# Infini-attention beside grouped attention: segment 3's memory is asked inside the attention, and the last q tile is split behind the flag

## The chip, the cores and the metric

The kernel runs on one core of a Trainium2 chip. The metric is the device time of one launch in microseconds, as the median of several runs; all matrices go in and come out in float32.

## What is computed

Two attention layers work on their own inputs, and their outputs are put side by side. Both have S = 2048 tokens, D = 576, 32 heads of 18.

```python
# A: all heads share one k and one v
scores = einsum("bhqd,bkd->bhqk", q, k) * Dh ** -0.5
a = merge(einsum("bhqk,bkd->bhqd", softmax(scores), v)) @ wo

# B: four segments of 512 tokens, causal inside a segment, with a memory of the segments before
phi = lambda t: where(t > 0, t + 1.0, exp(t))
for s in range(4):
    p = softmax(einsum("bhqd,bhkd->bhqk", qs, ks) * scale + mask)
    a_dot = einsum("bhqk,bhkd->bhqd", p, vs)
    num = einsum("bhld,bhde->bhle", phi(qs), M)              # the memory is asked
    den = einsum("bhld,bhd->bhl", phi(qs), z)[..., None] + 1e-6
    o = g * (num / den) + (1.0 - g) * a_dot
    M = M + einsum("bhld,bhle->bhde", phi(ks), vs)
    z = z + sum(phi(ks), "l")
b = merge(o) @ wo
```

Segment 0 has an empty memory. Segments 1, 2 and 3 ask it: a numerator of 18 values for each head and token, and a denominator.

## The kernel before, in words

**Two stages.** The first makes all projections: A in four chunks of 512 tokens, then B in four segments. Heads lie seven to a tile (126 rows; the fifth tile has four heads, 72 rows), so q of a segment is five tiles t = 0 to 4. Each result is split exactly into two parts (`split2`: a rounding cast on ScalarE, a subtraction on VectorE) and stored to DRAM (`store_parts`). The second stage is the attention, which loads stacks of eight heads back from DRAM. Between the two stands a branch on `flag`: if a bound on the scores is too loose, exact maxima are computed first. With these inputs that part is skipped, but each engine reads the flag and branches, and at the branch SP waits until all DMAs issued before it from the hardware queues are counted, for both ways have to leave the semaphores alike.

**The end of the first stage (segment 3, `last`).** For each q tile t = 0 to 3 (lines 527 to 539): project into one of four PSUM buffers `pj`, take the absolute value (`magnitude`), split, store to `qB`, then `phi` (Relu and Exp on ScalarE, one VectorE operation) and `from_memory`. Then come the denominators (541 to 550), the bound matmuls `pu` (554), the reduction to `fm` (555), `loose_flag`, the shifts (`shift_parts`, stored to `shB`), and `values(i, 1)`: the second half of v in four groups of 14 matmuls, each copied by ScalarE and stored to `vB` from ScalarE's queue. PE, ACT and DVE take these in the order that a scheduler gives them; `pin` and `keep_in_program_order` hold some where the program has them.

**Asking the memory.** There are two ways. Segment 3 asks in the first stage: `from_memory` multiplies `phi(q)` by the memory `Mst` (429), weighs the result by the gate (433) and stores it to `numB`; lines 545 to 550 make the denominators. Segments in `LATE_ASK`, (1, 2), only store `phi(q)` to `qfB` and their memory to `mzB` (426, 597, 598). In the attention `ask_memory` works them off: six pairs of steps for a segment (t = -1 for the denominators, then the five tiles), each step four matmuls of 256 columns on a 32-column strip (826) into the one PSUM buffer F. A pair ends with one or two VectorE reads (831, 835), and two turns later the stores to `numB` and `denB`. `asked[0]` says which segment is done.

**The attention's order** is written out by hand for PE, ACT and DVE. Work is cut into blocks of four heads, `("A", chunk, group)` or `("B", segment, group)`, and these into turns k of up to three items: 416 turns, 11 for a block of A, two for a block of B. In a turn stand the scores of three items (PE, 919 for A and 928 for B), their exponentials (ACT, 937; one of three from a copy W that VectorE makes, 934), one step of other work, and the products of the turn before the last (PE, 967). The step of other work is one of `ask_memory` until that is through, then one of the output projection (`run_fill`, 770):

```python
if memory is None:
    run_fill()
elif k >= ASK and all(its[n][0] == "A" for n, pr in turns[k]) and next(memory, None) is None:
    memory = None
```

So asks stand in turns of A only, from k = ASK = 20 on.

**Buffers and due times.** `later` is a list of steps with the turn from which they are due and a condition (`at`, `due`). The pool tile "o" has two buffers. `load_qf(s)` loads `phi(q)` of a segment into one, and the output projection's `parts` take the same two afterwards. `load_qf(1)` stands ahead of the turns, `load_qf(2)` is due at k = 24. `place()` lets a finished block take a buffer for its heads only once enough segments are asked. All loads and stores of the attention go through SP's queue, in order.

## Time and profile before

| | us |
|---|---|
| median of 3 runs | 1421.37 (1420.92 to 1422.42) |
| the profiled execution, its own time | 1422.46 |
| its span, from first to last instruction | 1420.8 |
| first score of the attention (PE) | 292.81 |
| busy in the span: PE / ACT / DVE / POOL | 1404.1 / 1205.0 / 1034.9 / 248.5 |
| mean granted clock of TensorE | 0.998 |

Times in rows are microseconds from the span's start. A row of the time line gives start, duration, engine, line, operation, output and input, count, and in brackets how long the engine had been idle and what released it. A row of groups gives the count, then the busy time in us and the mean of one in ns. A row of a stretch gives its bounds and length, the busy time of PE, weight loads, DVE, ACT and POOL with counts, the granted clock, the DMA share and GB/s. In a row of a line's instructions stand the shortest, median and longest duration in ns and the first and last start. Matmuls are pipelined, so their durations overlap; what one costs is read from starts.

### The profile page before, as it was taken

What the parts mean: (1) busy time and instruction counts of PE and PEld (TensorE: products, weight loads), DVE (VectorE), ACT (ScalarE), POOL (GpSimd) and SP (SyncE); (2) the same over time, 40 slices, a digit from 0 to 9 for tenths busy, and PEclk for the clock granted to TensorE, in tenths of its full rate; (3) what the DMA queues carried; (4) which work ended last, traced back from release to release, by engine and by line L of the source; (5) the groups of instructions that cost most, each with busy time, mean ns of one, the idle gap of its engine ahead of it and who ended that gap; (6) DMA issues with size and microseconds to landing.
All of it is one profiled execution on the core that took longest, in us unless ns stands there. A gap on an engine that the chain in (4) does not pass through costs nothing.

```text
span 1420.8 us, 40029 instructions
## 1 busy us (share of the span) xinstructions
PE 1404.1 (99%) x17132; PEld 844.8 (59%) x17132; DVE 1034.9 (73%) x1220; ACT 1205.0 (85%) x1448; POOL 248.5 (17%) x326
## 2 busy tenths in 40 slices
PE   9999999999999999999999999999999999999998
PEld 6788888745555555555555555555555555555558
DVE  6656456467787778877777888777778877887773
ACT  4543434479999999999999999999999999999991
POOL 2431000003313214221110160131011400100002
PEclk9999999999999999999999999999999999999999
DMA  9866546467565535332312542232104121110013
GB/s 271 268 207 187 166 144 219 168 175 223 154 212 160 168 117 162 90 113 77 111 58 70 165 131 91 67 107 75 51 34 135 64 75 47 59 44 18 9 60 111
DMA packets 90720, 172.63 MB, mean 122 GB/s; under 512 B 14576, under 2 KB 22889, under 8 KB 90110
## 3 DMA queue, kind: packets, MB, share of 16 engines
q1 hardware_dynamic: 83978, 159.75, 35.9%
q0 software_dynamic: 1664, 4.78, 1.3%
q10 hardware_dynamic: 4896, 5.51, 1.1%
q8 instruction: 135, 2.21, 0.7%
q14 instruction: 47, 0.39, 0.1%
HBM read 99.32 MB, written 70.67 MB: 120 GB/s over the span
## 4 chain that ended last, share of the span: by engine, by line
PE 67%; ACT 9%; issue 2%; DVE 1%; DMA 0%; POOL 0%; ACTq 0%; DVEq 0%
PE O L967 30%; PE E L919 19%; PE F L770 11%; ACT P L937 9%; PE E L928 3%; PE E L1164 2%; PE F L826 1%; DVE W L934 0%; DMA oA<-oe 0%; PE F L1164 0%; PE O L1164 0%; DMA sm<-oA 0%; POOL P L942 0%; DVE osb L794 0%; DVE o L831 0%
## 5 line engine op out<-in xcount | busy, mean ns | idle before, releaser
L937 ACT ACTIVATE P<-E 128x1024 f32<-128x1024 f32 (+1 forms) x800 | 781.7, 1062 | 11.7 <-PE E L919 11.6
L934 DVE COPY W<-E 128x1024 f32<-128x1024 f32 (+1 forms) x384 | 461.0, 1200 | 176.3 <-PE E L919 120.1
L967 PE MATMUL O<-P,VA 128*32 128x256 f32 x7936 | 508.3, 379 | 0.0
L937 ACT ACTIVATE P<-W 128x1024 f32<-128x1024 f32 (+1 forms) x384 | 427.9, 1114 | 3.9 <-DVE W L934 3.7
L967 PEld LDWEIGHTS O<-P,VA 128*32 128x32 f32 x7936 | 262.6, 110 | 146.5 <-issue 5.7
L919 PE MATMUL E<-stA,kstA 56*128 56x512 f32 x1920 | 329.0, 439 | 2.3 <-DVE W L934 1.3
L919 PEld LDWEIGHTS E<-stA,kstA 56*128 56x128 f32 x1920 | 154.9, 184 | 178.1 <-ACT P L937 112.4
L942 POOL TENSOR_SCALAR_AFFINE_SELECT P<-P 128x256 f32<-128x256 f32 (+1 forms) x192 | 94.6, 493 | 474.0 <-ACT P L937 441.5
L758 POOL TENSOR_TENSOR o<-o,rb 126x512 f32<-126x512 f32 (+1 forms) x55 | 81.9, 1504 | 410.2 <-DMA o<-oA 263.8
L770 PE MATMUL F<-woB,o 126*32 126x192 f32 (+1 forms) x1920 | 127.4, 338 | 0.3 <-DVE osb L794 0.3
L899 DVE SCALAR_TENSOR_TENSOR q<-q,PD 128x1024 f32<-128x1024 f32 x96 | 120.3, 1253 | 0.0
L967 PE MATMUL O<-P,vseg 128*32 128x256 f32 (+2 forms) x1536 | 81.8, 344 | 0.4 <-issue 0.3
L770 PEld LDWEIGHTS F<-woB,o 126*32 126x32 f32 (+1 forms) x1920 | 38.2, 108 | 70.7 <-issue 62.7
L976 DVE COPY oe<-O 128x512 f32<-128x512 f32 x64 | 44.2, 691 | 40.7 <-PE O L967 40.0
L249 PE MATMUL pj<-xh,wBl 128*126 128x512 f32 x180 | 72.4, 403 | 0.0
L249 PE MATMUL pj<-xh,wBh 128*126 128x512 f32 x180 | 71.8, 400 | 0.0
L118 ACT CAST qp<-pj 126x512 fp32r<-126x512 f32 (+1 forms) x54 | 30.9, 584 | 44.7 <-DVE kmB L447 32.9
L770 PE MATMUL F<-woA,o 126*32 126x192 f32 (+1 forms) x960 | 63.9, 338 | 0.0
L967 PEld LDWEIGHTS O<-P,vseg 128*32 128x32 f32 x1536 | 49.0, 109 | 24.9 <-issue 2.0
L928 PE MATMUL E<-stB 56*128 56x256 f32 (+3 forms) x512 | 61.2, 347 | 1.3 <-ACT P L937 0.9
L119 DVE TENSOR_TENSOR qp<-pj,qp 126x512 fp32r<-126x512 f32 (+1 forms) x54 | 36.6, 684 | 35.4 <-ACT qp L118 35.2
L249 PE MATMUL pj<-xl,wBh 128*126 128x512 f32 x144 | 57.3, 399 | 0.0
(193 smaller groups left out, 1388.6 us busy)
## 6 DMA issues: line engine op xcount, KB each, us to landing
stB<-kB SPq DMA_DIRECT2D x96, 144.0 KB
stB<-qB SPq DMA_DIRECT2D x32, 288.0 KB
stA<-qA SPq DMA_DIRECT2D x30, 288.0 KB
oA<-oe SPq DMA_DIRECT2D x32, 256.0 KB
oB<-oe SPq DMA_DIRECT2D x32, 256.0 KB
qA<-qp SPq DMA_DIRECT2D x16, 504.0 KB
kB<-qp SPq DMA_DIRECT2D x16, 504.0 KB
qB<-qp SPq DMA_DIRECT2D x16, 504.0 KB
```

The costliest lines, as they stand in the source:

```text
L119: hold(nc.vector.tensor_tensor(qp[:R, 1, :n], src, qp[:R, 0, :n].bitcast(F32), op=ALU.subtract))
L249: nc.tensor.matmul(dst, w[:, c0 : c0 + M], x, start=i == 0, stop=i == len(ops) - 1)
L758: return lambda: tc.keep_in_program_order(nc.gpsimd.tensor_tensor(dst, a, b, op=op))
L770: nc.tensor.matmul(dst[32 * j : 32 * j + 32], parts[ab, c][: RT[t], t, r0 : r0 + 32], wo[ab][: RT[t], t, c0 : c0 + n], start=start, stop=stop,
L899: steps.append(lambda a=a: v.scalar_tensor_tensor(q, q, a, p, op0=ALU.add, op1=ALU.mult))
L919: nc.tensor.matmul(e[:, j], kstA[rows, 128 * kt : 128 * kt + 128], st[rows, h, :], start=True, stop=True)
L928: nc.tensor.matmul(e[:, j, c0 : c0 + 512 - 128 * k], st[rows, 4 + h, ks], st[rows, h, 128 * k :], start=True, stop=True)
L934: nc.vector.tensor_copy(src[:, :, :n], e[:, :, :n])
L937: nc.scalar.activation(p[:, :, :n], src[:, :, :n], AF.Exp, scale=SCALE)
L942: nc.gpsimd.affine_select(diag, diag, pattern=[[0, 2], [0, m], [1, 128]], base=0, channel_multiplier=-1, compare_op=ALU.is_ge, fill=0.0)
L967: nc.tensor.matmul(o[32 * j : 32 * j + 32, q0 : q0 + n], v, p[:, j % 2, p0 : p0 + n], start=m == hf == 0, stop=last and hf == 1,)
L976: nc.vector.tensor_copy(osb, o)
```

## The change

Segment 3 joins `LATE_ASK`. It stores `phi(q)` in place of numerators, from POOL's queue instead of SP's; its matmuls, gate multiplications and denominators leave the first stage. In segment 3 the last q tile (t = 3) is only projected and its absolute value taken in the loop; its split, store, `phi` and `from_memory` come behind `loose_flag`.

In the attention 36 steps of `ask_memory` are worked off instead of 24. A turn may now take one if its items are of A, or if the products that it takes (of the turn two before) are of the same kind as its items. The third `load_qf` becomes due at k = 32 once segment 1 is asked, and is issued three turns later, into the buffer that segment 1's q had; the buffer's stores must have landed. `place()` lets the first finished block load its heads once two segments are asked, the second once three are.

```diff
-LATE_ASK, ASK = (1, 2), 20
+LATE_ASK, ASK = (1, 2, 3), 20
...
             def from_memory(t):
                 R = RT[t]
                 if s in LATE_ASK:
-                    nc.sync.dma_start(qfB[s][:R, t], fs[t][:R])
+                    (nc.gpsimd if last else nc.sync).dma_start(qfB[s][:R, t], fs[t][:R])
                     return
...
                 proj(pj[:126], wBh, wBl, xh, xl, 126 * t, 126)
                 magnitude(t, pj)
+                if last and t == 3:
+
+                    lastq = pj
+                    continue
                 qp = split2(pt, pj[:126], 126)
                 store_parts(qp, 0, 126, qB[s], 7 * t, 7)
...
             if last:
                 loose_flag()
+                qp = split2(pt, lastq[:126], 126, pin)
+                store_parts(qp, 0, 126, qB[s], 21, 7)
+                fs[3] = phi(lastq[:126], 126, "qf", 5, pin)
+                from_memory(3)
             sp = shift_parts(pt, pu, -BOUND_UP, C, 128)
             sent = nc.sync.dma_start(shB[s].rearrange("j r t -> r j t"), sp.bitcast(F32))
...
         def place():
 
-            return (ab, c) in parts or len(parts) - filled[0] // FILL < 2 and asked[0] >= min(2, len(parts) + 1)
+            return (ab, c) in parts or len(parts) - filled[0] // FILL < 2 and asked[0] >= min(3, len(parts) + 2)
...
         at(ASK + 4, 0, lambda: True, lambda k: load_qf(2))
 
+        at(ASK + 12, 0, lambda: asked[0] >= 1, lambda k: at(k + 3, 0, lambda: True, lambda k: load_qf(3)))
+
...
             if memory is None:
                 run_fill()
-            elif k >= ASK and all(its[n][0] == "A" for n, pr in turns[k]) and next(memory, None) is None:
+            elif k >= ASK and its[turns[k][0][0]][0] in ("A", its[prods[k - 2][0][0]][0]) and next(memory, None) is None:
+
                 memory = None
```

## The prediction

> **What bounds the kernel now.** I read the page's busy time and slices first, then stretches of the time line around the three places that the change touches.
>
> ```profile
> PE 1404.1 (99%) x17132; PEld 844.8 (59%) x17132; DVE 1034.9 (73%) x1220; ACT 1205.0 (85%) x1448; POOL 248.5 (17%) x326
> ...
> PE   9999999999999999999999999999999999999998
> ...
> ACT  4543434479999999999999999999999999999991
> ```
>
> Two stages stand there. Up to the eighth slice (some 290 us) PE is full and ACT half idle: the projections, bound by PE. From the ninth slice PE and ACT are both full: the attention, where one of them is the bound in each kind of turn and the other is close behind. The change takes PE work out of the end of the first stage and puts it into the second.
>
> **PE work that leaves the first stage.** Segment 3 loses five numerator matmuls (L429) and five denominator matmuls (L545).
>
> ```profile
> L429 PE MATMUL mm<-qf,Mst 126*126 126x512 f32 (+1 forms) x10 | 5.2, 602 | 0.0
> ...
> L545 PE MATMUL nd<-qf,zst 126*32 126x512 f32 (+1 forms) x10 | 3.4, 602 | 0.0
> ...
> L554 PE MATMUL nd<-aq,kbB 126*32 126x512 bf16 (+1 forms) x5 | 1.0, 386 | 0.0
> ```
> ```profile
> 274.27 0.39 PE L249 MATMUL pj<-xl,wBh 128*126 128x512 f32 x1
> ...
> 274.50 0.40 PE L249 MATMUL pj<-xh,wBl 128*126 128x512 f32 x1
> ...
> 274.74 1.02 PE L429 MATMUL mm<-qf,Mst 126*126 126x512 f32 x2
> ...
> 275.83 0.40 PE L249 MATMUL pj<-xl,wBh 128*126 128x512 f32 x1
> ...
> 285.22 1.05 PE L545 MATMUL nd<-qf,zst 126*32 126x512 f32 x4
> ...
> 286.20 0.27 PE L396 MATMUL nd<-ident,fm 128*1 128x128 f32 x1
> ```
>
> Matmuls overlap, so I price them by starts. Two projection steps take 2 x 0.23 (274.27 to 274.50); from 274.50 to 275.83 there are two of them and one L429, so an L429 holds PE for 1.33 - 0.46 = 0.87, and five for 4.35 us. Each is recorded as two rows, hence x10. Four of the ten L545 rows take 286.20 - 285.22 = 0.98; all ten at that rate 2.45. Together 6.8 us; the busy columns (5.2 + 3.4) cap it at 8.6, and 4.35 alone is the floor. VectorE loses six operations here, which nobody on this path waits for any more.
>
> **A wait that appears.** In the changed program's order the last q tile keeps its PSUM buffer until behind the flag, so the second group of `values` must take the buffer of the second q tile. That is free only after ScalarE has done four operations behind the last projection (absolute value, Relu, cast, Exp) and VectorE two.
>
> ```profile
> L388 DVE SCALAR_TENSOR_TENSOR qf<-pj,ph_e 126x512 f32<-126x512 f32 x5 | 3.4, 679 | 1.1 <-ACT ph_e L386 1.1
> L118 ACT CAST qp<-pj 126x512 fp32r<-126x512 f32 x6 | 3.3, 590 | 0.5 <-ACT kn L495 0.4
> L386 ACT ACTIVATE ph_e<-ph_e 126x512 f32<-126x512 f32 x5 | 3.1, 629 | 0.1
> ...
> L385 ACT ACTIVATE ph_e<-pj 126x512 f32<-126x512 f32 x5 | 3.0, 593 | 3.1 <-DVE qp L119 3.1
> ```
> ```profile
> 289.58 0.40 ACT L493 COPY vch<-pj 128x288 f32<-128x288 f32 x1 [1.47 <-PE pj L491]
> ...
> 290.01 0.33 ACTq L496 DMA_DIRECT2D vB<-vch  x1
> ...
> 291.12 0.29 PE L491 MATMUL pj<-wBl,xh 128*128 128x288 f32 x1
> ...
> 291.45 0.40 ACT L493 COPY vch<-pj 128x288 f32<-128x288 f32 x1 [1.47 <-PE pj L491]
> ...
> 292.81 1.16 PE L919 MATMUL E<-st,kstA 56*128 56x512 f32 x6 [1.41 <-SPq L607]
> ```
> ```profile
> L607 SPq EVENT_SEMAPHORE  x8: 17/17/17, 292.1 to 292.6; - x8
> ```
>
> The chain takes 0.59 + 0.59 + 0.59 + 0.63 (taking the absolute value as long as the Relu) and then 2 x 0.68, about 3.8 us. In it PE has one group of `values`, 1.87 us (copies at 289.58 and 291.45), and four of the five bound matmuls of L554, 0.8. So PE waits 1.1 us (0 to 1.8). Net on PE so far: 6.8 - 1.1 = 5.7 us earlier at its last `values`.
>
> **The handover.** The bracket at 292.81 says what released the attention: SP's eight semaphore events at the branch, 292.1 to 292.6. They follow stores: the third `vB` store went out at 290.01, so a store takes about 2.1 us to be counted. The fourth is issued behind the branch and holds nobody. Before, PE went idle at 291.41 and started at 292.81, 1.40 later. In the changed order all four `vB` stores stand ahead of the branch. Behind PE's end there now come the copy 0.40, the store 2.1, three events of 0.07 (eight took 0.5; this store counts on the sixth of the eight semaphores) and 0.2 to PE's start, with small gaps 2.95. That gives back 1.55: 5.7 - 1.55 = 4.1.
>
> SP's branch waits for other stores too: the last q tile and the shifts now leave behind the flag. By the built order the flag is written beside the third group of `values`, some 1.4 groups or 2.6 us ahead of the last `vB` store.
>
> ```profile
> 288.00:290.00 2.00, 2.00 (x17) 2.00 (x16) 0.00 (x0) 0.51 (x2) 0.00 (x0) 1.00 1.05 400
> ```
> ```profile
> qB<-qp SPq DMA_DIRECT2D x4, 504.0 KB
> ...
> vB<-vch ACTq DMA_DIRECT2D x5, 152.0 KB
> shB<-shp SPq DMA_DIRECT2D x1, 512.0 KB
> ```
>
> 504 + 512 + 3 x 152 and one `qfB` store (126x512 floats, 252 KB) make 1.72 MB. At 400 GB/s that is 4.3 us, against 2.6 + 2.1 = 4.7 to the count of the last `vB` store; with the start-up of the burst it lands 0 to 0.9 us later than that. I take 0.4, so the attention starts 3.7 us earlier (bounds: 2.5 and 5.2, the latter without wait and burst). `qfB` moves from SP to POOL. The Trainium skill (Trainium Kernel Development and Optimization, Key Constraints) says that the queues of SP, ACT and POOL run on the same 16 DMA engines. By that the 252 KB stay in the burst; with a path of its own for POOL it would be 0.6 us shorter. The DMA share of 1.05 in the row fits, but shows no POOL store.
>
> **The asks in the attention.** Twelve steps are added, four matmuls each. By the built order they stand so that eight more fall into turns of B and four more into turns of A, of which two had no step; the output projection starts two turns later and makes both up in turns that were empty, with the same three steps left at the end.
>
> ```profile
> 309.32 1.98 ACT L937 ACTIVATE P<-E 128x1024 f32<-128x1024 f32 x2
> ...
> 312.07 2.00 ACT L937 ACTIVATE P<-E 128x1024 f32<-128x1024 f32 x2
> ...
> 379.50 1.78 ACT L937 ACTIVATE P<-E 128x1024 f32<-128x1024 f32 x2
> ...
> 388.81 2.07 ACT L937 ACTIVATE P<-E 128x1024 f32<-128x1024 f32 x2
> 391.10 1.94 ACT L937 ACTIVATE P<-E 128x1024 f32<-128x1024 f32 x2 [0.22 <-PE E L919]
> ...
> 466.94 1.72 ACT L937 ACTIVATE P<-E 128x1024 f32<-128x1024 f32 x2
> ...
> 476.35 1.94 ACT L937 ACTIVATE P<-E 128x1024 f32<-128x1024 f32 x2
> 478.84 1.94 ACT L937 ACTIVATE P<-E 128x1024 f32<-128x1024 f32 x2 [0.55 <-PE E L919]
> ```
> ```profile
> 348.67 0.64 PE L826 MATMUL F<-o,woA 126*32 126x256 f32 x8
> 349.13 1.48 PE L967 MATMUL O<-P,VA 128*32 128x256 f32 x24
> ...
> 351.44 0.64 PE L826 MATMUL F<-o,woA 126*32 126x256 f32 x8
> ...
> 462.44 0.53 PE L770 MATMUL F<-woB,o 126*32 126x192 f32 x8
> 462.79 1.37 PE L967 MATMUL O<-P,vseg 128*32 128x256 f32 x24
> ```
>
> A turn of A lasts 312.07 - 309.32 = 2.75 without a step and 351.44 - 348.67 = 2.77 with an ask: 0.02 each, 0.1 for all. A pair of B turns without a step lasts (388.81 - 379.50) / 2 = 4.65, paced by ACT. With steps of the output projection, 0.35 each (462.44 to 462.79), it lasts (476.35 - 466.94) / 2 = 4.70, paced by PE, and ACT's gap at the next turn of A grows from 0.22 to 0.55. An ask holds PE for 0.46 (348.67 to 349.13), 0.11 more than those: the pair becomes 4.92, 0.27 over 4.65. Four pairs: 1.1. Two stretches end in a gap that is 0.2 to 0.3 longer: 0.5. Sum 1.7 us, bounds 0 (PE's lead covers all) and 12 x 0.46 = 5.5. VectorE takes seven more short reads of F beside its 27% idle time: nothing, up to 1 if they delay a copy that ACT waits for. The third q's load stands behind stores issued three turns earlier, so SP's queue, with the stacks behind it, waits for what has landed: nothing.
>
> **The clock.**
>
> ```profile
> 296.60:300.00 3.40, 3.40 (x26) 1.49 (x30) 3.40 (x4) 3.40 (x5) 0.00 (x0) 0.50 0.72 170
> ```
>
> The granted clock is 0.50 in these 3.4 us, soon after the gap, and ACT stays full. PE's gap now grows from 1.4 to some 3.3 us. A second such stretch would meet turns of which PE needs 2.77 - 0.46 = 2.31 at full clock, 4.62 at half, against 2.75: a loss of 3.4 x (1 - 2.75 / 4.62) = 1.4. I take 0.2 of 0 to 1.4. The Trainium skill (TensorE: Matmul & The Clock Gate, What's actually happening) has the clock halved after an idle window of about 3.4 us; by it a second slow window is possible here, not certain, and would cost that 1.4.
>
> **Sum.** -3.7 + 1.7 + 0.2 = -1.8 us. The profiled execution took 1422.46 (its span 1420.8 and 1.66 around it), 1.09 over the median of the three runs, so it would be 1420.7, and the median 1421.37 becomes 1419.6 us.
>
> **The rivals.** What a measurement of this kernel can tell from no change is about 0.2%, 2.84 us.
> Faster: the asks hide and the early work is worth all of its price. The start gains its bound 5.2, the asks cost 0.8: -4.4, 1417.0. For it: PE's own work in a pair is 4.70 - 0.70 = 4.0 of the 4.65. Against it: the 0.35 steps already show at 4.70.
> Slower: the handover becomes bound by transfers. If the 1.72 MB at the branch run at 200 GB/s instead of 400, they take 8.6 us, 4.3 more: the start gains -0.6, and with 1.7 and 0.2 the time is 1421.4 + 2.5 = 1423.9. It decides from 3.7 us more, that is below some 215 GB/s. Against it stand the 400 GB/s, with nearly the same stores; for it, that the burst is the largest of the stage and now stands directly ahead of the start.
> The change doing nothing of what it says is no rival: the built order has the matmuls moved.
>
> **How the numbers follow.** The forecast of -1.8, with terms that leave it within 2.84, gets 0.58. Faster gets 0.30, since 1 us less of wait, burst or asks suffices. Slower gets 0.12, with the load of the third q or the upper bound of the asks beside the burst. Range: the forecast's own terms reach from 1418 to 1422; stretched to the faster case's 1417.0 and towards 1423.9 it is 1416.8 to 1423.0.
>
> **What would show it.** Right: no L429 in segment 3's end, PE's first score near 289, its gap before it 3 us or more, released by SP's branch; B pairs with asks at 4.9. Wrong: the first score at 291 or later, B pairs still at 4.65, a long wait of PE for `qf`, or a slow clock stretch of 7 us.

## The result: 1425.4 us, 0.26% slower

| | before | after |
|---|---|---|
| median of 8 runs each, on one chip | 1421.3 (1420.8 to 1423.5) | 1425.4 (1422.2 to 1429.7) |
| ratio after / before, 95% interval | | 1.0026 (1.0016 to 1.0035) |
| profiled execution: own time / span | 1422.46 / 1420.8 | 1424.54 / 1422.8 |
| mean granted clock | 0.998 | 0.995 |

The forecast was 1419.6 with a range to 1423.0: the wrong sign, and outside the range. The page of the changed kernel, its busy time and two of its slices:

```profile
PE 1401.0 (98%) x17208; PEld 845.2 (59%) x17208; DVE 1036.2 (73%) x1221; ACT 1205.5 (85%) x1448; POOL 248.9 (17%) x331
...
PE   9999999989999999999999999999999999999998
...
PEclk9999999989999999999999999999999999999999
```

The totals do not say where the time went: PE is busy 3 us less in a span that is 2 us longer. The ninth slice of PE and of its clock, where the handover lies, has an 8. To see the rest one needs a ruler. VectorE's first operation on the scores of A (`PD<-E`, line 892 before, 900 after) starts each block of A. The table has its starts in both traces and the time since the start before. The last column has the names that the experiments use: the stretch from the first to the second start is the "first block", and each later stretch has the name of the start that ends it.

| start of block of A | before | after | after - before | time since the last, before | after | called in the experiments |
|---|---|---|---|---|---|---|
| 1 (turn 0) | 293.94 | 291.12 | -2.82 | | | |
| 2 (turn 19) | 340.65 | 338.85 | -1.80 | 46.71 | 47.73 | first block |
| 3 (turn 38) | 388.52 | 387.93 | -0.59 | 47.87 | 49.08 | third block |
| 4 (turn 53) | 427.58 | 430.40 | +2.82 | 39.06 | 42.47 | fourth block |
| 5 (turn 72) | 476.52 | 480.22 | +3.70 | 48.94 | 49.82 | fifth block |
| 32 | 1348.42 | 1352.30 | +3.88 | | | |

So 2.8 us are won at the start, 1.0 and 1.2 are lost in the next two stretches, 3.4 between turns 38 and 53, 0.9 behind that, and next to nothing more for 870 us. (The span grew by only 2.0 because the profiled execution of before took 1.9 us longer from start 32 to its end; the medians differ by 4.1, the last row of the table by 3.9.)

**1.45 of the 2.8 us are not the change's.** PE's first matmuls of the kernel stay longer at about half their later pace in some executions than in others. Before, and after:

```profile
6.77 2.06 PE L281 MATMUL pj<-xh,wAh 128*114 128x512 f32 x4 [1.21 <-ACT wAh L222]
8.62 0.63 PE L281 MATMUL mm<-xh,wAh 128*126 128x512 f32 x1
```
```profile
6.71 1.19 PE L281 MATMUL pj<-xh,wAh 128*114 128x512 f32 x4 [1.16 <-ACT wAh L222]
7.74 0.39 PE L281 MATMUL mm<-xh,wAh 128*126 128x512 f32 x1
```

Four matmuls take 1.85 us in the one (8.62 - 6.77) and 1.03 in the other, in the same order. From some 20 us up to 270 us, where the change begins, the traced execution of before is 1.1 to 1.5 us later at the same matmuls (191.38 against 189.93, for one). Call the one a late beginning and the other an early one. Both are found with both first stages among the kernels of the experiments. Between traces that begin alike, the changed stage has PE's last values 5.3 to 6.2 us earlier, the first score 2.1 to 3.3 and the first start 1.0 to 2.4: that is what the change wins at the start.

**The stretch that loses 3.4 us.** What the engines waited for between 300 and 484 us (in total, how often, the longest), before:

```profile
ACT P L937 <- DVE W L934: 1.0, 3, 0.4
```

and after:

```profile
ACT P L945 <- DVE W L942: 5.3, 3, 3.7
...
PE E L927 <- DVE W L942: 2.8, 3, 1.5
DVE sm L734 <- DMA sm<-oB: 2.6, 1, 2.6
...
PE F L834 <- DMA o<-qfB: 1.6, 1, 1.6
```

The time line of the changed kernel there, each engine's rows that have a wait, with the releaser in brackets:

```profile
411.35 0.64 PE L834 MATMUL F<-o,woA 126*32 126x256 f32 x8 [1.56 <-DMA o<-qfB]
...
412.88 0.95 DVE L734 RECIPROCAL sm<-sm 112x128 f32<-112x128 f32 x1 [2.63 <-DMA sm<-oB]
...
415.44 1.06 ACT L945 ACTIVATE P<-W 128x1024 f32<-128x1024 f32 x1 [3.72 <-DVE W L942]
...
415.46 0.50 PE L927 MATMUL E<-stA,kstA 56*128 56x512 f32 x2 [1.52 <-DVE W L942]
```

VectorE's order is written out by hand. In it the reciprocal of B's first sums waits for their load (2.63 us); behind the reciprocal stands the copy W that ScalarE's next exponential needs (3.72 us of waiting), and then TensorE has no free scores buffer (1.52 us). The chain of the changed kernel goes through the same load (start, us, what):

```profile
394.22 6.56 DMA stA<-qA
400.80 12.05 DMA sm<-oB
412.88 0.96 DVE sm L734
...
414.18 1.22 DVE W L942
```

SyncE's queue shows what is new ahead of it. Before:

```profile
395.22 0.40 SPq L880 DMA_DIRECT2D vseg<-vB  x1
396.90 0.86 SPq L713 DMA_DIRECT2D sm<-oB  x1
```

After:

```profile
396.09 0.83 SPq L888 DMA_DIRECT2D vseg<-vB  x1
397.55 0.34 SPq L811 DMA_DIRECT2D o<-qfB  x1
398.88 0.32 SPq L812 DMA_DIRECT2D o<-qfB  x1
400.80 1.93 SPq L721 DMA_DIRECT2D sm<-oB  x2
402.77 8.76 SPq L710 DMA_DIRECT2D woB<-b_wo  x5
```

The third q's load (1.15 MB) now stands between B's values (1.2 MB) and the sums (64 KB). Before the change the sums were issued 8.4 us after the third start (396.90 - 388.52), and VectorE took their reciprocal at 407.78 without a wait. After the change they were issued 12.9 us after that start, and took 12.05 us to land.

One more thing moved. The list of small steps takes at most two in a turn (`most=2` in `due`). In the changed kernel the third q's load takes one of the two places of turn 39, so the step that loads the sums goes from turn 39 to turn 40, and the reciprocal, five turns behind it, from turn 44 to 45. VectorE comes to it 22.3 us after the third start (412.88 - 2.63 - 387.93) where it came after 19.3 before the change (407.78 - 388.52). The later place gave the sums 3 us more time; the wait is what was left in spite of it.

**The start.** The changed handover, rows of PE and of ScalarE, then two stretches:

```profile
284.13 0.29 PE L491 MATMUL pj<-wBl,xh 128*128 128x288 f32 x1
...
284.89 0.73 ACTq L496 DMA_DIRECT2D vB<-vch  x1
...
288.94 0.46 PE L927 MATMUL E<-st,kstA 56*128 56x512 f32 x1 [4.52 <-DMA vB<-vch]
289.74 1.61 PE L927 MATMUL E<-st,kstA 56*128 56x512 f32 x5 [0.33 <-SPq L615]
...
290.81 3.88 ACT L945 ACTIVATE P<-E 128x1024 f32<-128x1024 f32 x4 [5.95 <-SPq L615]
```
```profile
284.00:286.00 2.00, 0.42 (x4) 0.18 (x2) 0.00 (x0) 0.40 (x1) 0.00 (x0) 1.00 0.99 334
286.00:288.00 2.00, 0.00 (x0) 0.00 (x0) 0.00 (x0) 0.00 (x0) 0.00 (x0) 1.00 1.00 320
```

PE ends 7.0 us earlier (284.4 against 291.4), the first score comes 3.9 earlier, the first exponential 2.7 (293.55 before), each with the 1.45 in it. Between the end of PE's work and the first score the transfer engines are full (shares 0.99 and 1.00) at 320 to 334 GB/s.

### The profile page after: what moved, and what is told of

Same layout as the page of the kernel before. It is cut to its first block, busy times and chain, and to the rows that moved or that the text cites. A ratio compares the mean times of both kernels' runs of the same rounds, so it can differ in the third digit from the quotient of the medians.

```text
span 1422.8 us, 40185 instructions
## 1 busy us (share of the span) xinstructions
PE 1401.0 (98%) x17208; PEld 845.2 (59%) x17208; DVE 1036.2 (73%) x1221; ACT 1205.5 (85%) x1448; POOL 248.9 (17%) x331
## 4 chain that ended last, share of the span: by engine, by line
PE 67%; ACT 7%; issue 2%; DMA 2%; DVE 1%; SPq 1%; ACTq 0%; DVEq 0%
PE O L975 31%; PE E L927 19%; PE F L778 11%; ACT P L945 7%; PE E L936 3%; PE E L1175 2%; DMA sm<-oB 1%; PE F L834 1%; DMA stB<-qB 0%; DMA stA<-qA 0%; DVE W L942 0%; PE F L1175 0%; PE O L1175 0%; SPq L701 0%; SPq L847 0%
## 5 line engine op out<-in xcount | busy, mean ns | idle before, releaser
L984 DVE COPY oe<-O 128x512 f32<-128x512 f32 x64 | 44.2, 691 | 39.8 <-PE O L975 37.6
L118 ACT CAST qp<-pj 126x512 fp32r<-126x512 f32 (+1 forms) x54 | 31.0, 584 | 45.3 <-DVE kmB L447 33.1
L119 DVE TENSOR_TENSOR qp<-pj,qp 126x512 fp32r<-126x512 f32 (+1 forms) x54 | 36.6, 685 | 35.6 <-ACT qp L118 35.6
```

Of the source, the lines that this page charges most:

```text
L119: hold(nc.vector.tensor_tensor(qp[:R, 1, :n], src, qp[:R, 0, :n].bitcast(F32), op=ALU.subtract))
L984: nc.vector.tensor_copy(osb, o)
```

## The experiments

Theory 1: the third q's load makes B's sums late, and VectorE's order passes that on. Rival 1: the asks, in turns of B above all, cost TensorE the time. Rival 2: the longer pause at the handover costs clock. All numbers of blocks are from one profiled execution each, which can lie some us beside the median of its kernel; the medians are of 4 to 12 runs. The kernels ran on several chips, on which the kernel before had medians from 1421.2 to 1422.1; the ratios are each to before on the same chip. Of the traces in the table, before, "no third load" and "asks held" have the late beginning, the others the early one. "Keys" is the issue of the last piece of B's next keys on SyncE's queue, counted from the fourth start; it is explained further below.

| kernel | median | ratio to before (95%) | first start | first | third | fourth | fifth block | keys |
|---|---|---|---|---|---|---|---|---|
| before | 1421.3 | | 293.94 | 46.71 | 47.87 | 39.06 | 48.94 | 25.9 |
| after | 1425.4 | 1.0026 (1.0016-1.0035) | 291.12 | 47.73 | 49.08 | 42.47 | 49.82 | 33.1 |
| early q | 1428.6 | 1.0060 (1.0041-1.0078) | 291.41 | 47.32 | 49.08 | 45.33 | 48.98 | 29.9 |
| late sums | 1422.4 | 1.0010 (1.0000-1.0021) | 290.80 | 47.59 | 49.08 | 40.53 | 48.98 | 34.6 |
| two segments, asks in B | 1421.3 | 1.0004 (0.9995-1.0014) | 292.91 | 47.00 | 49.12 | 38.98 | 48.30 | 26.8 |
| no third load | 1423.5 | 1.0010 (1.0001-1.0020) | 292.96 | 47.57 | 49.13 | 39.76 | 49.49 | 32.5 |
| early q, late sums | 1425.4 | 1.0029 (1.0016-1.0042) | 291.18 | 47.73 | 49.12 | 39.12 | 52.94 | 36.5 |
| weights late | 1425.3 | 1.0025 (1.0013-1.0036) | 290.53 | 47.79 | 49.10 | 40.03 | 49.83 | 35.6 |
| late sums, weights late | 1422.7 | 1.0009 (0.9995-1.0024) | 290.96 | 47.74 | 49.10 | 39.56 | 49.38 | 35.3 |
| the same, asks held | 1428.3 | 1.0044 (1.0031-1.0056) | 292.48 | 47.67 | 49.10 | 38.75 | 56.84 | 39.8 |
| q on GpSimd's queue | 1426.5 | 1.0029 (1.0018-1.0040) | 291.17 | 47.74 | 49.11 | 44.06 | 49.67 | 32.5 |
| the same, late sums | 1426.2 | 1.0026 (1.0015-1.0037) | 291.69 | 47.37 | 49.10 | 39.03 | 55.83 | 38.7 |
| sums two turns late | 1424.6 | 1.0019 (1.0010-1.0028) | 291.15 | 47.21 | 49.09 | 41.18 | 48.84 | 33.1 |
| the same, weights late | 1428.1 | 1.0048 (1.0034-1.0062) | 291.12 | 47.74 | 49.10 | 40.00 | 53.08 | 37.0 |

**The reciprocals three turns later (late sums).**

```diff
-... (2, 5, 3, 5) if (ab, c) == ("B", 0) ...
+... (2, 8, 3, 5) if (ab, c) == ("B", 0) ...
```

> The load of B's first sums stays where it is, and the reciprocals that read them are asked of VectorE three turns later. Theory 1: VectorE's wait at the reciprocal (2.6 us) and the waits of ScalarE on W (3.7) and TensorE on W (1.5) in 410 to 416 us go; what stays is TensorE's 1.6 us for the q of the asks. The fourth block's loss falls from 3.4 to about 1.5 us, the time to about 1423.3. Rivals 1 and 2: no part of the loss hangs on the reciprocal, 1425 stays.

Measured: 1422.4, 3.0 under the changed kernel by the medians, 2.3 by the ratios. VectorE has no wait at the reciprocal, the fourth block is 40.5, and TensorE's wait for q is what is left:

```profile
PE F L834 <- DMA o<-qfB: 1.6, 1, 1.6
```

As theory 1 said, and neither rival: only the reciprocal, the deadline of the sums, was moved, with the steps that follow from it.

**No third load.**

```diff
+        if s == 3:
+            nc.gpsimd.memset(qfs[s], 1.0)
+            return
         nc.sync.dma_start(qfs[s][:126, :4], qfB[s][:126, :4])
```

> Leaves out part of the computation: the third segment's q is not loaded (1.15 MB less on SyncE's queue), GpSimd fills the tile with ones in its place, and everything else, the asks too, is as in the changed kernel. Theory 1 as the first runs leave it (wherever the load stands ahead of the sums, its bytes and its turn on SyncE's queue make the sums late): the load of the sums lands some 6 us after its issue and not after 12, VectorE does not wait at the reciprocal, TensorE does not wait for q, and the fourth block's loss of 3.4 us falls under 0.5; about 1421.5. Rival 1 (the asks themselves, in turns of B and in the third segment, cost TensorE the time): at most the 1.6 us of the wait for q goes, 1423.8 or more.

Measured: no wait at the reciprocal and none for q, and the fourth and fifth block together are 4.3 - 1.25 = 3.0 us shorter than after's. The sums are issued 9.4 us after the third start, though their step stands in turn 40 here too: of the 4.5 us by which the changed kernel issued them later, the load itself made 3.5. The median is 1423.5, 2 us over the expectation. (The trace has the late beginning, which says nothing of the median: PE's last values start at 285.83 and not 284.13, with the same order of matmuls.) So the load costs 1.9 us by the medians, 2.3 by the ratios, and without it the change would still not pay: 1.0010 (1.0001 to 1.0020). The 36 asks run in full here, so rival 1 has at most 1.25 of the 4.3 us.

**Two segments, asks in turns of B.** The kernel before with the new condition of turns alone:

```diff
-elif k >= ASK and all(its[n][0] == "A" for n, pr in turns[k]) and next(memory, None) is None:
+elif k >= ASK and its[turns[k][0][0]][0] in ("A", its[prods[k - 2][0][0]][0]) and next(memory, None) is None:
```

> The kernel before with only the new condition of turns: its two segments ask B's memory in turns of B too; no third q, first stage untouched. Rival 1: the asks in turns of B by themselves cost their time on TensorE beyond what they displace, about 1.2 us (6 asks), so 1422.5. Theory 1: no cost that is not the load's: no wait of VectorE for the sums over 0.5 us, the same time as before within 0.5 us (1421.3).

Measured: the same time, 1.0004 (0.9995 to 1.0014). The third block is 1.25 us longer, by six asks, and the fourth and fifth are 0.7 us shorter, since fewer are left for them. Asks in turns of B take 0.2 us each (1.25 / 6), and 0.7 of the 1.25 comes back; rival 1 falls as an explanation of 4 us. (This trace has the early beginning, so that its first start is 1.0 us earlier than before's with the same first stage.)

**The third q's load three turns earlier (early q).**

```diff
-at(ASK + 12, 0, lambda: asked[0] >= 1, lambda k: at(k + 3, 0, lambda: True, lambda k: load_qf(3)))
+at(ASK + 12, 0, lambda: asked[0] >= 1, lambda k: load_qf(3))
```

> The third q's load (1.2 MB) is put on SyncE's queue three turns earlier, ahead of the values' load and not between it and the load of the sums. Theory 1 (the load sits right before the sums of B, whose landing then takes 12 us; VectorE waits for them at the reciprocal, and behind that stand the copies W that ScalarE's next exponential needs): the wait of VectorE at the reciprocal goes from 2.6 us to under 0.5, the stretch from the third to the fourth block loses 0 to 1 us against before in place of 3.4, and the time is about 1422.0 us. Rival 1 (the asks in turns of B cost TensorE its time) and rival 2 (the longer pause at the handover costs clock): the stall is by chance beside that load, nothing of the loss goes, 1425.

Measured: 1428.6, three us worse. TensorE no longer waits for q, and VectorE waits longer:

```profile
DVE sm L734 <- DMA sm<-oB: 4.0, 1, 4.0
```

A miss, and not for the reason that comes to mind first. Here the third q's load leaves turn 39, so the reciprocal is back in turn 44. VectorE's rows ahead of it, here:

```profile
405.32 1.21 DVE L907 SCALAR_TENSOR_TENSOR q<-q,PD 128x1024 f32<-128x1024 f32 x1
410.57 0.95 DVE L734 RECIPROCAL sm<-sm 112x128 f32<-112x128 f32 x1 [4.03 <-DMA sm<-oB]
```

and in the changed kernel, where a copy W, two reads of F and this row stand between the same two:

```profile
409.55 0.69 DVE L909 TENSOR_SCALAR n<-n 128x1024 int32<-128x1024 f32 x1
```

VectorE comes to the reciprocal 18.7 us after the third start in place of 22.3. The sums are issued later than in the changed kernel (14.4 us after the third start, behind values that the load makes late), and yet they land sooner, 22.8 us after it in place of 24.9. So moving the load did bring the sums forward by 2.2 us; what was lost is the later deadline, 3.6 us. Theory 1 had to be put wider: 1.15 MB more anywhere ahead of the sums makes them late, and the wait is their landing less their deadline.

**Both together.** The two edits above in one kernel.

> The early load of the third q and the late reciprocals together. If it is the deadline of the sums that decides, the wait of 4.0 us that the early load alone showed at the reciprocal is covered by the three turns, and TensorE's wait of 1.6 us for q goes as well: fourth block's loss under 0.5 us, 1421.0, under the late reciprocals alone (1422.4). If the early load costs by what it does to the other loads ahead of it (the states of A, the values), it stays over 1423.

Measured: 1425.4. The fourth block is as before the change (39.1), as expected, and the fifth takes 52.9, 4 us longer than before. TensorE has a new wait of 2.2 us for B's next queries: the gain moved on. What that is, the runs further below show.

**Queue or room.** First the output projection's weights, queued behind the sums, ten turns later:

```diff
-load_wo(*(("B", b_wo) if it[2] == 2 else ("A", a_wo)))
+if it[2] == 2:
+    at(k + 10, 0, lambda: True, lambda k: load_wo("B", b_wo))
+else:
+    load_wo("A", a_wo)
```

> The changed kernel; only the five loads of the output projection's weights (1.3 MB, issued right behind the load of the sums, needed 20 turns later) are put ten turns later. Theory 1a, order: the sums are late because the third q's 1.15 MB and the values stand ahead of them, and what is queued behind them does not matter: the load still takes 12 us, VectorE waits 2.6 us at the reciprocal, the fourth block loses its 3.4 us, 1425. Theory 1b, room: all loads in flight share the engines, and 3.6 MB between 396 and 416 us are too many: with 1.3 MB gone the sums land in 7 to 8 us and q 2 us sooner, the waits at the reciprocal and for q fall under 1 us each, the fourth block loses under 1 us, 1422.5.

Measured: in the profile the sums land 10.0 us after their issue in place of 12.05, just in time,

```profile
409.92 0.95 DVE L734 RECIPROCAL sm<-sm 112x128 f32<-112x128 f32 x1 [0.18 <-DMA sm<-oB]
```

and the fourth block loses 1.0. But that execution took 1421.85, the least of ten; their median is 1425.3. With the sums 0.2 us from too late, most executions seem to fall on the other side, which no trace here shows. Undecided. Then the load went off SyncE's queue, with its bytes and its turn kept. Theory 2a is that the place in SyncE's queue makes the sums late, 2b that the bytes in flight do:

```diff
-        nc.sync.dma_start(qfs[s][:126, :4], qfB[s][:126, :4])
-        nc.sync.dma_start(qfs[s][: RT[4], 4], qfB[s][: RT[4], 4])
+        q = nc.gpsimd if s == 3 else nc.sync
+        q.dma_start(qfs[s][:126, :4], qfB[s][:126, :4])
+        q.dma_start(qfs[s][: RT[4], 4], qfB[s][: RT[4], 4])
```

> The changed kernel; only the third q's load goes through GpSimd's queue in place of SyncE's, at the same turn, when GpSimd stands idle (392 to 420 us). Theory 2a (SyncE's queue: it issues in order, and each issue waits for the landing of one some eight issues earlier, so that a long load ahead delays the issue of all that follow): the sums are issued some 8.5 to 9.5 us after the third block's start as before the change, not 12.9, VectorE does not wait at the reciprocal, the fourth block loses 0.5 to 1.5 us, 1422.5. Theory 2b (the room of the transfer engines): the same bytes fly in the same stretch, the sums land as late, the wait of over 2 us at the reciprocal stays, 1425.

Measured: 1426.5. GpSimd issues the load at 394.63, ahead of the values (395.93), where SyncE had issued it behind them. The first sums are issued 10.2 us after the third start, 2.7 sooner than in the changed kernel, and they land no sooner:

```profile
398.21 11.23 SPq L721 DMA_DIRECT2D sm<-oB  x2
```
```profile
413.17 0.95 DVE L734 RECIPROCAL sm<-sm 112x128 f32<-112x128 f32 x1 [2.31 <-DMA sm<-oB]
```

From 398.21 to some 413 are 15 us, and VectorE waits 2.3. Between the two loads of sums, SyncE's queue itself waits for a store of B's outputs to land:

```profile
SPq L721 <- DMA oB<-oe: 9.7, 1, 9.7
```

So 2a fails and it is as 2b said: what is in flight holds the sums, and not only the place in SyncE's queue. (The values were ahead of them on that queue in both kernels.) The Trainium skill (DMA: Bandwidth & Descriptors, Queues, rings and completion order) says that a transfer's count lands only after every earlier write of that DMA engine, across its queues. The trace agrees as far as it goes: 56 KB from SyncE's queue were counted 15 us after their issue, with 1.15 MB of another queue and 1.2 MB of their own in flight.

**Later deadlines and more room.**

Late reciprocals (three turns) and late weights in one kernel:

> The late reciprocals and the late loads of the weights together. By 1b q lands in time too, and TensorE's 1.6 us for it, which the late reciprocals alone left, go: fourth block under 0.5 us later than before's, 1421.0 and so about even with the kernel before. By 1a q still lands 13 us after its issue and the 1.6 us stay: 1422.4 as with the late reciprocals alone.

Measured: 1422.7, as the late reciprocals alone (1422.4). TensorE's wait for q falls from 1.6 to 0.7 in the profile; the time does not show it. To these two edits comes a hold of the third segment's asks:

```diff
         for s in LATE_ASK:
+            while s == 3 and now[0] < 48:
+                yield False
             qf = qfs[s]
```

> As the run before, and the third segment's asks are held until turn 48 (two turns later). If q is what TensorE still waits for, the hold takes the rest of that wait away whatever the loads do: no wait of TensorE for q over 0.3 us, 1420.5 to 1421.5, the fastest of the versions. If the hold only moves the asks to where they cost the same, it equals the run before.

Measured: 1428.3. The wait for q is gone and the fourth block is the shortest of all, 38.75; the fifth takes 56.8.

The load on GpSimd's queue with the reciprocals three turns late:

> The third q's load on GpSimd's queue and the reciprocals three turns later. By both theories there is no wait at the reciprocal; what the late reciprocals alone left was 1.6 us of TensorE for q. By 2a q is issued and lands sooner, and B's queries, behind it on SyncE's queue, too: 1421.0 to 1421.7, even with the kernel before. By 2b it is as the late reciprocals alone, 1422.4.

Measured: 1426.2, again with a fourth block as before the change (39.0) and a fifth of 55.8. Then the reciprocals two turns late, q on SyncE's queue:

```diff
-... (2, 5, 3, 5) if (ab, c) == ("B", 0) ...
+... (2, 7, 3, 5) if (ab, c) == ("B", 0) ...
```

> The changed kernel with B's first reciprocals two turns later in place of three. The wait was 2.6 us, a turn is about 2.5 us: if the slack of the sums is all that counts, two turns cover it as three did, and the store of the reciprocals, ahead of most of B's next queries on SyncE's queue, goes out one turn sooner: 1421.8 to 1422.4. If three turns had only by chance a good order on that queue, B's queries come late here, the fifth block is over 50 us, and the time 1424 or more.

Measured: 1424.6; the profiled execution, with 1422.15 the least of eleven, has no wait at the reciprocal and 2.1 us for q. Two turns seem too few for most executions, which no trace here shows. With the weights late as well:

> The same with the output projection's weights loaded ten turns later as well. Theory 2b (room): the sums and q land sooner, no wait at the reciprocal and under 1 us for q: 1421.5. If room does not matter once the sums have slack, it equals the run before.

Measured: 1428.1, the fifth block 53.1.

**What the fifth block waits for.** In the kernel with q on GpSimd's queue and late sums, TensorE:

```profile
466.89 0.47 PE L937 MATMUL E<-stB 56*128 56x512 f32 x1 [1.10 <-DMA stB<-kB]
470.04 1.51 PE L937 MATMUL E<-stB 56*128 56x512 f32 x5 [2.68 <-DMA stB<-ones_d]
```

These are the scores of turn 64, whose queries and keys SyncE's queue loads behind the third segment's stores and the inverses. The last piece was issued, before the change, after it, and in this kernel:

```profile
453.44 0.25 SPq L694 DMA_DIRECT2D stB<-ones_d  x1
```
```profile
463.53 0.25 SPq L702 DMA_DIRECT2D stB<-ones_d  x1
```
```profile
465.93 0.25 SPq L702 DMA_DIRECT2D stB<-ones_d  x1
```

That is 25.9, 33.1 and 38.7 us after the fourth start, the column "keys" of the table. Up to 35.6 the fifth block takes 48.3 to 49.8 us; at 36.5, 37.0, 38.7 and 39.8 it takes 52.9, 53.1, 55.8 and 56.8. Before the change there were some 10 us of cover (time by which a load may slip before anybody waits), and the change takes 7 of them. Four of the edits that delay the sums or the asks by two or three turns take the rest. They trade the fourth block against the fifth.

**The load wholly ahead of the stretch.**

```diff
-LATE_ASK, ASK = (1, 2, 3), 20
+LATE_ASK, ASK = (1, 2, 3), 16
```

> The changed kernel with one number changed: the asks begin at turn 16 in place of 20, so that the third q is loaded at turn 33 (about 372 us) in place of 39, ahead of the stretch from 396 to 416 us in which the values, the sums and the weights are loaded; the same 36 asks, four more of them in turns of B. Theory 1 (the loss is the third q's load meeting that stretch): SyncE's queue there is before's again, the sums land in 6 to 8 us, no wait at the reciprocal and none of TensorE for q, fourth and fifth block within 0.5 us of before's 39.1 and 48.9; about 1421.0, 4.3 under the changed kernel and even with or under the kernel before. Rival 1 (the asks of a third segment cost this wherever their q is loaded): over 1424.

Measured: 1433.9 (ratio 1.0081, 1.0061 to 1.0101). The asks now begin before the memory is there,

```profile
339.94 1.08 PE L834 MATMUL F<-o,woA 126*32 126x256 f32 x8 [6.35 <-DMA woA<-mzB]
```

so that the first block takes 56.8. And the fourth still takes 44.3, with 3.6 us at the reciprocal, though the load was issued at 389.0, nine us ahead of the third start. A miss, with the same trap as the early load: the load no longer takes a place in turn 39, and VectorE comes to the reciprocal 19.3 us after the third start, as before the change. The sums land 22.9 us after it, 2 us sooner than in the changed kernel. That they are not there sooner still may be the second segment's numerators (1.0 MB), which are now stored right behind the first sums; this store was not tried by itself. The same with turns 32 to 37 left without asks:

> As the run before, and turns 32 to 37 (of B, in the third block) are left without asks. If asks in turns of B cost 0.2 us each, as the third block's 1.2 us for six of them say, that block goes back to 47.9 us. By theory 1 the six asks then come later and q is still there in time: 1 us under the run before if the turns of A take them for nothing, the same if they cost there what they cost here. Two steps of the output projection are left for the end, about 1 us against it.

Measured: 1434.1 (ratio 1.0084, 1.0070 to 1.0099). In the profile the third block takes 48.6 in place of 48.9, the first is 2.7 us shorter, the fourth and fifth together 1.6 longer. The time is that of the run before: not worth 1 us.

**The handover.** 18 unread matmuls behind the last values:

```diff
+                pz = ps.tile([128, C], F32, name="nd", bufs=2)
+                for _ in range(18):
+                    nc.tensor.matmul(pz, wBh[:, 0, :128], wBh[:, 0, :512], start=True, stop=True)
```

> The changed kernel with 18 matmuls added that nobody reads, after the last values of the first stage, about 4.2 us of TensorE that stand in the pause before the branch. Rival 2 (the pause of 4.5 us makes the granted clock fall to 0.5 for 8 us of the first block, which loses 1.0 us): the slow stretch shrinks to before's 3.4 us or goes, and the time falls by about 1 us to 1424.4. Theory 1: the stall of 3.4 us at the fourth block stays whatever the clock does, so at most that 1 us is won.

Measured: 1429.0 (ratio 1.0052, 1.0035 to 1.0069), the first start at 297.08. Inconclusive: with so much PE work the automatic order put SyncE's first load of the attention ahead of the branch, where it waits for GpSimd's stores and the branch for it. With 11 of them SyncE's loads stay behind the branch:

> The changed kernel with 11 matmuls added that nobody reads, behind the last values of the first stage: 2.6 us of TensorE in its pause of 4.5 us before the first scores. Rival 2 (a pause of some length makes the granted clock fall to 0.5, and the longer pause is what costs the first block 1.0 us): the pause is then 1.9 us, near before's 1.4, the slow stretch comes later and is 3 to 5 us in place of 9, the first block takes 46.7 us in place of 47.7, and the time falls by 1.0 to 1424.4. If the clock follows something else than the pause, the slow stretch and the block stay. The stall of 3.4 us in the fourth block stays by either.

Measured: 1426.0 (1.0029, 1.0016 to 1.0042). The pause is 2.0 us, as expected. The first score comes at 291.02, against 290.75 in the kernel without the third load, which has the late beginning as this one has (last values at 286.2 here and 285.8 there), and in both PE waits for a `vB` store. So the burst of stores sets the start, not PE. The granted clock (before the last two numbers) from 284 to 304 us, before, after, and here:

```profile
284.00:304.00 20.00, 17.45 (x134) 10.40 (x136) 12.57 (x18) 11.84 (x16) 0.53 (x1) 0.91 0.55 162
```
```profile
284.00:304.00 20.00, 14.43 (x110) 6.85 (x110) 10.81 (x10) 12.77 (x15) 0.15 (x1) 0.74 0.55 155
```
```profile
284.00:304.00 20.00, 16.20 (x116) 9.52 (x118) 10.05 (x10) 11.86 (x15) 0.67 (x2) 0.83 0.59 163
```

Of 20 us at full clock (1 - 0.91) x 20 = 1.8, 5.2 and 3.4 were lost: one, three and two stretches of 3.4 us at half. The number of stretches alone does not order the first blocks: 46.7, 47.7 and 47.5 in these three, 47.2 to 47.9 in the others with three. What orders them is how much of the half clock lies behind the first start, for where a stretch falls differs from one execution to another. Read in steps of half a microsecond, in the traces of this case (but for the two whose asks begin at turn 16, where the first block waits for the memory):

| half clock behind the first start, us | traces | first block |
|---|---|---|
| 3.4 | before; two segments | 46.7, 47.0 |
| 6.8 to 7.1 | sums two turns late; 11 matmuls; early q; q on GpSimd's queue, late sums | 47.2, 47.5, 47.3, 47.4 |
| 7.3 to 7.8 | 18 matmuls; late sums; no third load; asks held | 47.6, 47.6, 47.6, 47.7 |
| 8.3 to 8.9 | after; early q, late sums; weights late; late sums, weights late; q on GpSimd's queue; two turns, weights late; tail in its loop | 47.7 to 47.9 |

From 3.4 to 8.4 us the block grows by 1.0, 0.2 us for each microsecond, and the same first stage is found in three of the four rows. In the changed kernel the whole 1.0 has come about by 8.6 us after the first start, where the half clock ends. So rival 2 has the 1.0 us of the first block, and nothing of the 3.4. These are single traces, and but for the added matmuls it was chance that moved the half clock, no edit.

**The last tile halved in its loop again.**

```diff
-                if last and t == 3:
-                    lastq = pj
-                    continue
...
-                qp = split2(pt, lastq[:126], 126, pin)
-                store_parts(qp, 0, 126, qB[s], 21, 7)
-                fs[3] = phi(lastq[:126], 126, "qf", 5, pin)
-                from_memory(3)
```

> The last tile of q is halved in its loop again, as before; three segments are still asked in the attention. If the move of the tile behind the flag is what lets TensorE's values come up (so that its last values end 7 us earlier than before), the start of the first block moves back by 0.5 to 2 us and the time rises to 1426 to 1427. If the move only serves the order of the stores, the start stays within 0.5 us, and 1425.4 stays. The stall of the fourth block is the same by both.

Measured: 1425.1 (1.0022, 1.0012 to 1.0032), no different from 1425.4 with the tail. The values start their last matmul at 285.91 and the first start is 293.07, 1.9 us later than after's. But this trace has the late beginning; in four others with it and with the tail behind the flag the two are at 285.4 to 285.8 and 292.5 to 293.0. The tail's part of the change is worth at most 0.6 us at the start, and nothing that the medians can tell.

No version that asks three segments in the attention is under the kernel before. The best, the reciprocals three turns later, is at 1422.4, 1.0010 (1.0000 to 1.0021).

## Why the prediction was wrong

Three terms failed: the third q's load, put at nothing, cost some 2 to 3 us; the start was won 1 to 2.4 us earlier in place of 3.7; the clock cost 1.0 in place of 0.2. The first is the largest, but without it the sum would have been too low as well: the kernel without the load is at 1423.5.

- **PE work that leaves, 6.8 less a wait of 1.1.** PE's last values end 7.0 us earlier where 5.7 were forecast. Of these 1.45 are the early beginning; between traces that begin alike it is 5.3 to 6.2. A wait of 0.6 us came in place of 1.1. This term was right.
- **Handover and burst.** 1.55 and 0.4 were given back in the forecast, so that the start came 3.7 earlier. All four `vB` stores do stand ahead of the branch and release the first score. That it came at 288.94, near the 289 forecast, is luck: 1.45 of it are the early beginning, and five traces with the late one have it at 290.3 to 291.0. The burst ran at 320 to 334 GB/s and not 400, and SyncE's branch was through only at 290.7, on which ScalarE waited: the first exponential is 2.7 earlier, the first block of A 2.8, or 1.0 to 2.4 between traces that begin alike. The term was some 2 us too large.
- **The asks.** ScalarE's exponentials in turns of B with asks, two pairs apart:

```profile
377.71 1.78 ACT L945 ACTIVATE P<-E 128x1024 f32<-128x1024 f32 x2
...
387.76 1.94 ACT L945 ACTIVATE P<-E 128x1024 f32<-128x1024 f32 x2
```

A pair takes (387.76 - 377.71) / 2 = 5.03 where 4.92 was forecast, and the third block loses 1.2 us, where 1.7 was forecast for all. Right in mechanism, and by the run with two segments in good part paid back later.
- **"The third q's load stands behind stores issued three turns earlier, so SP's queue, with the stacks behind it, waits for what has landed: nothing."** This is the step that failed. It asked what the load waits for, and not what the load does to what follows it. The sums behind it were issued 12.9 us after the third start in place of 8.4, and landed 12 us after their issue; VectorE's order turned that into 3.4 us. Moving the sums' deadline by three turns gave back 3.0 us, taking the load away left 1.25 of the 4.3 us in the fourth and fifth block, and the load on another queue still cost them. The nothing put down for VectorE ("up to 1 if they delay a copy that ACT waits for") fell with it: ScalarE waited 3.7 us for one copy, delayed not by the reads of F but by the sums. The sign "a long wait of PE for `qf`" came too, with 1.6 us.
- **The clock.** 0.2 was taken of 0 to 1.4; the first block lost 1.0. The mechanism was right and the size was not: 10 us at half clock, 8.4 of them behind the first start, where one stretch of 3.4 was added as the worst case. The prediction had named 7 us as a sign against it. Its upper bound, 1.4 for 3.4 us, is 0.4 for each microsecond at half clock; 0.2 were measured.
- **The rivals.** The slower one was placed at the branch, as a burst of transfers at 200 GB/s; the burst ran at 320 to 334. Transfers that hold what starts next were the largest part of the loss, but 110 us later, where 3.6 MB of loads (values, third q, weights) meet a small one with a deadline. That the time came out on the slower side is no merit of that reason.

## What to carry to other kernels

A load that is added in a busy stretch is to be costed by the small transfers that land behind it: find the next one that an in-order engine waits for, and its slack in the trace of before. Here no wait at all was recorded there before the change, and an issue 4.5 us later with a landing of 12 us cost 3.4. Before a difference of starts in two traces is read, align them at an instruction that the change does not touch: here half of the gain at the start was there after 20 us. Where steps share a fixed number of places in a turn, look also at what a new step pushes on, and what a moved one lets slip back: the early load brought the sums 2.2 us forward and their deadline 3.6. And a deadline that is moved moves the next ones: count the cover of what is queued behind as well, before moving anything by turns.

## What the runs showed of the hardware

- Taking a 1.15 MB load off SyncE's queue to GpSimd's, and so ahead of the 1.2 MB of values, let a 56 KB load be issued 2.7 us sooner and land as late (15 us after its issue in place of 12).
- PE's first four matmuls of line 281 took 1.85 us in some executions and 1.03 in others, and the difference of some 1.5 us stayed to the end of the stage.
- A microsecond at half clock behind the first start cost the first block of A 0.2 us (0 to 1.1 us of loss between 3.4 and 8.9 us at half).
- Half clock came in whole stretches: read in steps of half a microsecond, what was lost at the handover was 1.71 us in the kernel before, 3.42 with 11 filling matmuls, 5.12 in most others and 6.83 in one, one to four times half of 3.41 us. A pause of PE of only 1.4 us was enough for one. The Trainium skill (TensorE: Matmul & The Clock Gate, What's actually happening) has a free-running window of 3413 ns, which agrees with the steps. That it takes an idle window to halve the clock does not fit as it stands: 1.4 us of pause, with two gaps of 0.65 and 0.41 behind it, is not an idle window of 3.4.
